# A two-slope rectifier in place for narrowing float64 weights, and 128 columns instead of 80 in the stationary operands of counts and means

## The chip, the core and the metric

The kernel runs on one core of one Trainium2 chip. The time is that of one execution on the device, in microseconds (us); smaller is better.

The names used for the engines: PE is TensorE (matrix multiplications; its weight loads are listed apart as PEld), DVE is VectorE, ACT is ScalarE, POOL is GpSimd, SP is SyncE, which here only issues DMA transfers. SBUF is the on-chip working memory, PSUM the small memory that PE writes its results into.

## The reference

Three stages follow each other. The first is an attention over 16 (batch, head) pairs of 768 positions and 64 dimensions, in which a query sees only the keys of its own cluster. A query whose cluster has no key gets the mean of v. The second is a gated feed-forward layer, the third a soft mixture of experts.

```python
q_assign = np.argmax(np.einsum('bhsd,hcd->bhsc', q_n, c_n), axis=-1)
k_assign = np.argmax(np.einsum('bhsd,hcd->bhsc', k_n, c_n), axis=-1)
mask = q_assign[:, :, :, None] == k_assign[:, :, None, :]
scores = np.where(mask, scale * np.matmul(q, k.transpose(0, 1, 3, 2)), -1000000000.0)
attn = np.exp(scores - np.max(scores, axis=-1, keepdims=True))
attn = attn / (np.sum(attn, axis=-1, keepdims=True) + 1e-09)
x = np.matmul(attn, v)                       # reshaped to 1536 x 512
...
h = x @ w_in                                 # 1536 x 2048
g = h * np.clip(h + 3.0, 0.0, 6.0) / 6.0
x = g @ w_out
...
logits = x @ phi                             # dispatch and combine by softmax of logits,
h = np.maximum(slot_input[e] @ w1[e], 0.0)   # 8 experts with 4 slots each
slot_out[e] = h @ w2[e]
```

`w_in` (512 x 2048) and `w_out` (2048 x 512) reach the kernel as float64, two 32-bit words a number. PE multiplies float16 and float32, so the kernel first narrows them to float32.

## The kernel before, in words

The work is written as generators that yield at places where another step may come in between; the table `ORDER` (lines 29 to 132) says by number which generator goes on next. All engines thus get one fixed sequence of instructions, and each engine works through its own strictly in that order. A second table, `ROOMS`, gives each tile its buffer.

**Attention, heads 0 to 15.** For each head: q and k are loaded and split into a high and a low float16 half (`cast_hi`, `cast_lo`), clusters are found (`as_mm`, `as_max`; the one-hot rows of keys and queries stand in the tile `oh`), the row maxima are taken from a first product (`maxq` on PE, line 531, then `maxr` on DVE, line 547, and `shift`, lines 554 and 556), the scores are formed (`scores`, lines 569 and 573), exponentiated on ACT (`exps`, lines 610 and 617), split (ACT line 342, POOL line 352, which the helpers `high` and `low` issue) and multiplied by v (`pv`, lines 639, 644, 645 and 652).

**Counts and means** (`cnt_mm`, lines 497 to 525), once for each head. Six products count the keys of each cluster (line 505: the stationary operand is a stretch of 5 x 16 = 80 columns of `oh`, the moving one a column of ones), and twelve form the mean of v (lines 507 and 508: the stationary operand is `wmean`, 80 columns, zero but for the last 16). Only rows 64 to 79 of the result are read.

**Narrowing** (`narrow`, lines 870 to 891), for 16 pieces of 128 x 1024 numbers: 8 of `w_in` (tile `wi`, through `win`) and 8 of `w_out` (tile `wod`, through `wout`). A piece lies in a buffer of `ring_a` (4 buffers), low and high words alternating. Its steps:

- part 0: DVE masks the sign out of the high words into the tile `nw` (line 878); ACT takes the absolute value of the high words, seen as float32, times 2 to the -111, into a PSUM tile `nt` (line 880). `nt` takes one of the three two-bank buffers of PSUM that the scores, maxima and hidden products also use.
- part 1: DVE shifts `nt` left by 3 and ors in the sign (line 883).
- part 2: DVE shifts the low words right by 29, ors in `nt` and writes the float32 (line 888). For `w_in` that is in place, then ACT and POOL split it (`wq`); for `w_out` it goes to `wo`, from which ACT issues a DMA (line 935), and the buffer of the piece is then free for the next load (line 922, on SP).

**The rest.** The hidden products (`hid`, line 710) of the first batch are interleaved with the attention of the second; after the attention its buffers are given to the experts' weights (`wk`), whose transfers run until the end.

The `consts` steps (lines 309 to 338) fill constants on POOL at the start.

Of the kernel before, what the change touches and what calls it, by code (L numbers as in the profile page):

```python
# [8 lines left out]
F16 = mybir.dt.float16  # L9
F32 = mybir.dt.float32  # L10
U32 = mybir.dt.uint32
I32 = mybir.dt.int32
AF = mybir.ActivationFunctionType
ALU = mybir.AluOpType
# [3 lines left out]
P = 128  # L18
# [213 lines left out]
def clustered_attention_ffn_softmoe(ctx: ExitStack, tc, q, k, v, cent, w_in, w_out, phi, w1, w2, out):  # L232
    nc = tc.nc
    B, H, S, D = q.shape
    C = cent.shape[1]
    NT = S // P
# [11 lines left out]
    cp = Rooms(ctx.enter_context(tc.tile_pool(name="cp", bufs=1, side="left")))  # L248
# [6 lines left out]
    ap = Rooms(att.enter_context(tc.tile_pool(name="ap", bufs=2, side="left")))  # L255
# [5 lines left out]
    def psm(nm):  # L261
        return ps_m.tile([P, 512], F32, tag="m", name=nm)

    def pss(nm):
        return ps_s.tile([P, 2, 512], F32, tag="s", name=nm)
# [17 lines left out]
    ident16 = cp.tile([P, P], F16, name="ident16")  # L283
    i4 = cp.tile([P, NS], F32, name="i4")
    ones = cp.tile([P, 1], F16, name="ones")
    wmean = cp.tile([P, 80], F16, name="wmean")
    rank = cp.tile([P, C], F32, name="rank")
    b_relu = cp.tile([P, 1], F32, name="b_relu")
    wp2 = cp.tile([P, NF, 2 * NS], F16, name="wp2")
# [11 lines left out]
    v32s = [ap.tile([P, NT, 65], F32, name=f"v32_{i}", bufs=1) for i in range(3)]  # L301
    mxs = [ap.tile([P, 96 + NT], F32, name=f"mxs_{i}", bufs=1) for i in range(2)]
    mvs = [ap.tile([P, 129], F16, name=f"mv_{i}", bufs=1) for i in range(3)]

    def second():
        nc.scalar.activation(sm.tile([P, 1], F32, tag="nm", name="warm_1", bufs=4), b_relu, AF.Exp)
        yield

    def consts():
        make_identity(nc, ident)  # L310
        nc.gpsimd.tensor_copy(ident16, ident)  # L311
        yield
        for c in range(C):
            nc.gpsimd.memset(rank[:, c : c + 1], float(C - c))
        yield
        for t in qk2:
            nc.gpsimd.memset(t[:, :, :, 80:128], 0.0)
            nc.gpsimd.memset(t[:, :, 1, 96 : 96 + NT], SH)
            yield
# [144 lines left out]
    def as_max(i):  # L464

        d = st[i]
        sc = d.pop("as")
        rk = rank.unsqueeze(1).to_broadcast([P, 12, C])
        nc.vector.tensor_tensor(out=sc, in0=sc, in1=rk, op=ALU.mult)
        yield  # L470
        mx2 = sm.tile([P, 12], F32, tag="mx2", name=f"mx2_{i}", bufs=2)
        nc.vector.tensor_reduce(out=mx2, in_=sc, op=ALU.max, axis=AX.X)
        oh = ap.tile([P, 2, NT, C], F16, tag="oh", name=f"oh_{i}")
        nc.vector.tensor_tensor(
            out=oh.rearrange("p a n c -> p n a c"),
            in0=sc.rearrange("p (n a) c -> p n a c", a=2),
            in1=mx2.rearrange("p (n a) -> p n a", a=2).unsqueeze(3).to_broadcast([P, NT, 2, C]),
            op=ALU.is_equal,
        )
        d["oh"] = oh  # L480
# [16 lines left out]
    def cnt_mm(i):  # L497

        d = st[i]
        oh = d["oh"]  # L500
        v1 = v1s[i % NV]
        pm = psm(f"cm_{i}")
        for n in range(NT):
            k5 = oh.rearrange("p a n c -> p (a n) c")[:, NT + n - 4 : NT + n + 1].rearrange("p n c -> p (n c)")
            nc.tensor.matmul(pm[0:80, 400:401], k5, ones, start=(n == 0), stop=(n == NT - 1))
        for n in range(NT):
            nc.tensor.matmul(pm[0:80, 0:65], wmean, v1[:, n, 0:65], start=(n == 0), stop=False)
            nc.tensor.matmul(pm[0:80, 0:64], wmean, v1[:, n, 65:129], start=False, stop=(n == NT - 1))
        yield
        emp = sm.tile([P, 1], F32, tag="emp", name=f"emp_{i}", bufs=2)  # L510
        nc.vector.tensor_scalar(out=emp[64:80], in0=pm[64:80, 400:401], scalar1=0.5, scalar2=None, op0=ALU.is_lt)
        yield
        d["cm"] = pm
        mv = mvs[i % 3]
        nc.vector.tensor_scalar(
            out=mv[64:80, 0:65], in0=pm[64:80, 0:65], scalar1=emp[64:80], scalar2=None, op0=ALU.mult
        )
        nc.vector.scalar_tensor_tensor(  # L518
            out=mv[64:80, 65:129],
            in0=pm[64:80, 0:64],  # L520
            scalar=emp[64:80],
            in1=mv[64:80, 0:64],
            op0=ALU.mult,
            op1=ALU.subtract,
        )
# [307 lines left out]
    def centroids():  # L833
        c32 = ap.tile([P, D], F32, tag="acp", name="c32", bufs=1)
        nc.scalar.dma_start(out=c32, in_=cent.rearrange("h c d -> (h c) d"))
        nc.gpsimd.memset(b_relu, 3.0 * SG)
        nc.scalar.activation(sm.tile([P, 1], F32, tag="nm", name="warm_0", bufs=4), b_relu, AF.Sqrt)
        yield
        sq = ap.tile([P, D], F32, tag="oh", name="csq")
        ss = sm.tile([P, 1], F32, tag="tm", name="css")  # L840
        nc.scalar.activation(sq, c32, AF.Square, accum_out=ss)
        y = sm.tile([P, 1], F32, tag="tm", name="cy")
        nc.scalar.activation(y, ss, AF.Sqrt)
        yield
        nc.vector.tensor_scalar(out=y, in0=y, scalar1=1e-20, scalar2=None, op0=ALU.max)
        r = sm.tile([P, 1], F32, tag="tm", name="cr")
        nc.vector.reciprocal(r, y)
        nc.vector.scalar_tensor_tensor(out=y, in0=ss, scalar=r, in1=y, op0=ALU.mult, op1=ALU.add)
        nc.vector.tensor_scalar(out=y, in0=y, scalar1=0.5, scalar2=1e-6, op0=ALU.mult, op1=ALU.add)
        nc.vector.reciprocal(r, y)  # L850
        cn = ap.tile([P, D], F32, tag="oh", name="cn")
        nc.vector.tensor_scalar(out=cn, in0=c32, scalar1=r, scalar2=SQ, op0=ALU.mult, op1=ALU.mult)
        cin = ap.tile([P, 4, D], F16, tag="ms", name="cin", bufs=1)
        cb = cn.unsqueeze(1).to_broadcast([P, 2, D])
        nc.vector.tensor_copy(cin[:, 0:2], cb)
        nc.vector.tensor_tensor(out=cin[:, 2:4], in0=cb, in1=cin[:, 0:2], op=ALU.subtract)
        yield
        tp = psm("ctp").bitcast(F16)[:, 0 : 2 * P].rearrange("p (a q) -> p a q", a=2)
        for a in range(2):
            nc.tensor.transpose(tp[:, a], cin[:, 2 * a : 2 * a + 2].rearrange("p a d -> p (a d)"), ident16)  # L860
        yield
        nc.vector.tensor_copy(ct, tp)
# [4 lines left out]
    raw = {}  # L867
    wo = {}

    def narrow(dst, src, nm, part):  # L870

        lo, hi = src[:, :, 0], src[:, :, 1]
        if part == 0:
            t = raw[nm, "t"] = pss(f"nt_{nm}").rearrange("p a b -> p (a b)").bitcast(U32)
            s = raw[nm, "s"] = ap.tile([P, 1024], U32, tag="nw", name=f"nw_{nm}", bufs=1)
            nc.vector.tensor_scalar(out=s, in0=hi, scalar1=0x80000000, scalar2=None, op0=ALU.bitwise_and)
            yield
            nc.scalar.activation(t.bitcast(F32), hi.bitcast(F32), AF.Abs, scale=2.0**-111)  # L880
        elif part == 1:
            t = raw[nm, "t"]
            nc.vector.scalar_tensor_tensor(
                out=t, in0=t, scalar=3, in1=raw.pop((nm, "s")), op0=ALU.logical_shift_left, op1=ALU.bitwise_or
            )
        else:
            t = raw.pop((nm, "t"))
            nc.vector.scalar_tensor_tensor(
                out=dst.bitcast(U32), in0=lo, scalar=29, in1=t, op0=ALU.logical_shift_right, op1=ALU.bitwise_or
            )  # L890
        yield

# [163 lines left out]
    def phs_load():  # L1056
        nc.sync.dma_start(out=phs, in_=phi.rearrange("(k p) s -> p k s", p=P))
        yield

    ev(consts)  # L1060
    for n in range(7):
        ev(keep, n, 4)
    ev(centroids)
    ev(load, 0, 0)
    ev(load, 0, 1)
# [4 lines left out]
    for i in range(NH):  # L1070
        if i == H:
            for t in range(NT):
                ev(xtrans, t)
        if i >= 2:
            ev(load, i, 0)
        if i:
            ev(load, i, 1)
        for fn in (cast_hi, cast_lo, as_mm, as_max, as_put, castv_hi, castv_lo, cnt_mm):
            ev(fn, i)
        for n in range(NT):  # L1080
            ev(maxq, i, n)
            ev(maxr, i, n)
        ev(shift, i)
        for t in range(NT):
            ev(scores, i, t)
            ev(exps, i, t)
            ev(plow, i, t)
            ev(pv, i, t)
        ev(finish, i)
        ev(split_x, i)  # L1090
# [387 lines left out]
```

## Time and profile before

| What | Value |
|---|---|
| Time, median of 3 runs | 478.05 us (477.79 to 480.21) |
| The profiled execution, first to last instruction (its span; no other time of it is recorded) | 475.5 us |
| PE busy | 437.2 us, 92% |
| ACT busy | 316.9 us, 67% |
| DVE busy | 284.3 us, 60% |
| POOL busy | 251.1 us, 53% |
| Chain that ended last, by engine | PE 66%, DVE 14%, ACT 8%, DMA 6% |

The profile follows one execution on the chip. Busy times are shares of the whole span, so they average stages that have different limits; a change in one stage is read from that stage. The chain of waits goes back from the last instruction, at each step to what released it or to the instruction before it on its engine. The ends of matrix products are modelled, so a PE that looks busy may still wait in part; the starts show the pace.

### The profile page before, as it was taken

Reading aid. Unit: us, or ns where it says so; the run is one execution under the profiler, and the core shown is the slowest. Engines: PE = TensorE matmul, PEld = TensorE weight load, DVE = VectorE, ACT = ScalarE, POOL = GpSimd, SP = SyncE. Lnnn points to the kernel's source line nnn. Section 1 sums busy time; section 2 is a strip of 40 time slices with the busy share of each in tenths; the row PEclk is TensorE's granted clock in tenths of the full one; section 3 lists DMA queues with packets and bytes.
Section 4 is the critical chain, followed back from the end, with each engine's and each line's share of the span. In section 5 each row is a group of like instructions: output and inputs, shape, how many; then the busy total and the mean of one; then the engine's idle time right before and its main releaser. Section 6 shows DMA issues by size and latency. Waiting matters only on the chain.

```text
span 475.5 us, 11894 instructions
## 1 busy us (share of the span) xinstructions
PE 437.2 (92%) x4938; PEld 283.1 (60%) x4938; DVE 284.3 (60%) x497; ACT 316.9 (67%) x518; POOL 251.1 (53%) x227
## 2 busy tenths in 40 slices
PE   6779999999979999999999998989998999789973
PEld 5557678777767656656666666754545545442443
DVE  4899999998968387466667759513233223540222
ACT  7369899898965978876789998963545335600121
POOL 5326588785644555666698897984313233130000
PEclk9789999999999999999999999999999999999998
DMA  8777866946794689689473555005996799999998
GB/s 280 187 150 187 193 172 174 271 122 196 244 253 113 177 203 195 139 157 226 112 145 72 54 102 139 3 1 106 314 307 207 158 274 373 406 341 384 339 284 272
DMA packets 133813, 95.50 MB, mean 201 GB/s; under 512 B 96384, under 2 KB 119424, under 8 KB 133760
## 3 DMA queue, kind: packets, MB, share of 16 engines
q1 hardware_dynamic: 129088, 88.95, 71.2%
q10 hardware_dynamic: 4672, 5.80, 3.4%
q8 instruction: 38, 0.62, 0.5%
q14 instruction: 15, 0.12, 0.1%
HBM read 64.06 MB, written 7.34 MB: 150 GB/s over the span
## 4 chain that ended last, share of the span: by engine, by line
PE 66%; DVE 14%; ACT 8%; DMA 6%; issue 3%; POOL 2%; SPq 0%; ACTq 0%; DVEq 0%; POOLq 0%
PE h L710 26%; DVE mxs L547 4%; PE st L569 4%; PE sm L531 4%; PE st L573 4%; PE e L1345 3%; DMA wod<-in_moe_w_out_dram 3%; PE acc L639 2%; PE acc L652 2%; PE z L819 2%; DMA wk<-in_moe_w_dram 2%; ACT p L617 2%; PE acc L645 2%; PE acc L644 2%; PE o L1382 2%
## 5 line engine op out<-in xcount | busy, mean ns | idle before, releaser
L352 POOL TENSOR_TENSOR pp<-p,pp 128x768 f16<-128x768 f32 x72 | 119.7, 1667 | 56.1 <-ACT pp L342 28.0
L710 PE MATMUL h<-wq,xt 128*128 128x512 f16 x576 | 132.1, 379 | 0.0
L547 DVE TENSOR_REDUCE mxs<-sm 128x1 f32<-128x768 f32 x96 | 89.5, 952 | 15.7 <-PE sm L531 15.0
L710 PEld LDWEIGHTS <-xt 128*128 128x128 f16 x576 | 55.2, 98 | 62.0 <-issue 2.5
L352 POOL TENSOR_TENSOR ghl<-r,ghl 128x1024 f16<-128x1024 f32 (+1 forms) x25 | 50.4, 2017 | 61.1 <-ACT ghl L342 55.9
L617 ACT ACTIVATE p<-st 128x768 f32<-128x768 f32 x72 | 57.9, 805 | 15.2 <-PE st L573 13.7
L342 ACT ACTIVATE pp<-p 128x768 f16<-128x768 f32 x72 | 60.3, 842 | 1.4 <-PE acc L652 0.2
L569 PE MATMUL st<-qk1t 128*128 128x384 f16 x192 | 47.6, 329 | 5.5 <-ACT p L617 4.9
L531 PE MATMUL sm<-qk2t 80*128 80x384 f16 x192 | 45.9, 331 | 2.7 <-DVE mxs L547 0.9
L729 DVE SCALAR_TENSOR_TENSOR r<-r,h 128x1024 f32<-128x1024 f32 (+1 forms) x26 | 29.5, 1135 | 31.4 <-ACT r L727 31.3
L573 PE MATMUL st<-qk2t 102*128 102x384 f16 x192 | 47.5, 329 | 0.0
L727 ACT ACTIVATE r<-h,b_relu 128x1024 f32<-128x1024 f32 (+1 forms) x26 | 27.2, 1045 | 24.7 <-PE h L710 13.8
L645 PE MATMUL acc<-v,pp 128*128 128x64 f16 x432 | 36.1, 194 | 0.0
L644 PE MATMUL acc<-v,pp 128*128 128x65 f16 x432 | 36.1, 192 | 0.0
L352 POOL TENSOR_TENSOR qk<-qk,qk 128x768 f16<-128x768 f32 x15 | 24.7, 1645 | 21.7 <-ACT qk L342 20.5
L639 PE MATMUL acc<-v,pp 128*128 128x65 f32 x288 | 35.8, 274 | 0.3 <-DVE wp L973 0.2
L639 PEld LDWEIGHTS acc<-v,pp 128*128 128x128 f32 x288 | 34.6, 192 | 1.5 <-DVE mv L518 0.3
L342 ACT ACTIVATE ghl<-r 128x1024 f16<-128x1024 f32 (+1 forms) x26 | 25.7, 989 | 14.3 <-DVE r L729 10.5
L644 PEld LDWEIGHTS <-pp 128*128 128x128 f16 x432 | 31.2, 99 | 2.5 <-ACT pp L342 0.2
L645 PEld LDWEIGHTS <-pp 128*128 128x128 f16 x432 | 29.2, 96 | 2.1
L342 ACT ACTIVATE qk<-qk 128x768 f32<-128x768 f32 (+2 forms) x32 | 26.2, 817 | 1.8 <-DMA qk<-in_k_dram 0.9
L361 PE MATMUL kw<-ident,ident 128*128 128x256 f16 x136 | 23.4, 306 | 4.0 <-POOL ident L311 1.8
(195 smaller groups left out, 785.3 us busy)
## 6 DMA issues: line engine op xcount, KB each, us to landing
wk<-in_moe_w_dram SPq DMA_DIRECT2D x60, 512.0 KB, 8.2
wi<-in_moe_w_in_dram SPq DMA_DIRECT2D x16, 512.0 KB, 5.7
wod<-in_moe_w_out_dram SPq DMA_DIRECT2D x16, 512.0 KB, 5.2
wos<-wo ACTq DMA_DIRECT2D x8, 512.0 KB, 3.2
wk<-wos SPq DMA_DIRECT2D x8, 512.0 KB, 6.6
qk<-in_q_dram SPq DMA_DIRECT2D x16, 192.0 KB, 3.0
qk<-in_k_dram SPq DMA_DIRECT2D x16, 192.0 KB, 3.5
v<-in_v_dram SPq DMA_DIRECT2D x16, 192.0 KB, 3.5
```

The lines of the kernel that those rows point to most:

```text
L342: nc.scalar.activation(out, in_, AF.Copy, scale=scale)
L352: (nc.vector if e == "v" else nc.gpsimd).tensor_tensor(out=out, in0=in_, in1=hi, op=ALU.subtract)
L531: nc.tensor.matmul(s[:, j, 0:384], d["qk2t"][0:80, n, 0], d["qk2t"][0:80, 3 * j : 3 * j + 3, 1], start=True, stop=True,)
L547: nc.vector.tensor_reduce(out=mxs[i % 2][:, 96 + n : 97 + n], in_=s[:, :, 0:384], op=ALU.max, axis=AX.XY)
L569: nc.tensor.matmul(s[:, j, 0:384], d["qk1t"][:, t, 1], d["qk1t"][:, 3 * j : 3 * j + 3, 0], start=True, stop=False)
L573: nc.tensor.matmul(s[:, j, 0:384], d["qk2t"][0 : 96 + NT, t, 1], d["qk2t"][0 : 96 + NT, 3 * j : 3 * j + 3, 0], start=False, stop=True,)
L617: nc.scalar.activation(p32, s[:, :, 0:384], AF.Exp, scale=sc_exp)
L639: nc.tensor.matmul(o, p32[:, j, r * P : (r + 1) * P], d["v32"][:, t], start=(t == 0 and n == 0), stop=False)
L644: nc.tensor.matmul(o, hi, v1[:, t, 0:65], start=(t == 0 and n == 0), stop=False)
L645: nc.tensor.matmul(o[:, 0:64], hi, v1[:, t, 65:129], start=False, stop=False)
L710: nc.tensor.matmul(s[:, fb % 2], xt[:, lhs], wq[fb][:, hl, kk], start=(n == 0), stop=(n == 11))
L729: nc.vector.scalar_tensor_tensor(out=g, in0=r, scalar=6.0 * SG, in1=sf, op0=ALU.min, op1=ALU.mult)
```

## The change

`narrow` loses the tiles `nw` and `nt` and one DVE instruction of three. Part 0 is now a shift of the low words right by 29 in place on DVE, and a two-slope rectifier (`Prelu`) of the high words in place on ACT, with the scale 2 to the -111 and the slope 2 to the 32 for negative inputs: the factor adds 32 to the exponent field, a bit that the later shift by 3 brings to the place of the sign. Part 1 does nothing. Part 2 shifts the high words left by 3 and ors in the low ones. `cnt_mm` uses stationary operands of 128 columns: the one-hot rows lie in two fixed tiles `ohs` with four zero groups behind the twelve, and `wmean` is 128 wide. POOL zeroes these with two more `memset`s. `ORDER` is not touched.

```diff
-    wmean = cp.tile([P, 80], F16, name="wmean")
+    wmean = cp.tile([P, P], F16, name="wmean")
...
+    ohs = [ap.tile([P, 16, C], F16, name=f"ohs_{i}", bufs=1) for i in range(2)]
...
             nc.gpsimd.memset(rank[:, c : c + 1], float(C - c))
+        for t in ohs:
+            nc.gpsimd.memset(t[:, 12:16], 0.0)
...
-        oh = ap.tile([P, 2, NT, C], F16, tag="oh", name=f"oh_{i}")
+        oh = ohs[i % 2][:, 0:12].rearrange("p (a n) c -> p a n c", a=2)
...
-        oh = d["oh"]
+        oh = ohs[i % 2]
         v1 = v1s[i % NV]
         pm = psm(f"cm_{i}")
         for n in range(NT):
-            k5 = oh.rearrange("p a n c -> p (a n) c")[:, NT + n - 4 : NT + n + 1].rearrange("p n c -> p (n c)")
-            nc.tensor.matmul(pm[0:80, 400:401], k5, ones, start=(n == 0), stop=(n == NT - 1))
+            k8 = oh[:, NT + n - 4 : NT + n + 4].rearrange("p n c -> p (n c)")
+            nc.tensor.matmul(pm[:, 400:401], k8, ones, start=(n == 0), stop=(n == NT - 1))
         for n in range(NT):
-            nc.tensor.matmul(pm[0:80, 0:65], wmean, v1[:, n, 0:65], start=(n == 0), stop=False)
-            nc.tensor.matmul(pm[0:80, 0:64], wmean, v1[:, n, 65:129], start=False, stop=(n == NT - 1))
+            nc.tensor.matmul(pm[:, 0:65], wmean, v1[:, n, 0:65], start=(n == 0), stop=False)
+            nc.tensor.matmul(pm[:, 0:64], wmean, v1[:, n, 65:129], start=False, stop=(n == NT - 1))
...
-        sq = ap.tile([P, D], F32, tag="oh", name="csq")
+        sq = ap.tile([P, D], F32, tag="csq", name="csq", bufs=1)
...
-        cn = ap.tile([P, D], F32, tag="oh", name="cn")
+        cn = ap.tile([P, D], F32, tag="cn", name="cn", bufs=1)
...
         if part == 0:
-            t = raw[nm, "t"] = pss(f"nt_{nm}").rearrange("p a b -> p (a b)").bitcast(U32)
-            s = raw[nm, "s"] = ap.tile([P, 1024], U32, tag="nw", name=f"nw_{nm}", bufs=1)
-            nc.vector.tensor_scalar(out=s, in0=hi, scalar1=0x80000000, scalar2=None, op0=ALU.bitwise_and)
+            nc.vector.tensor_scalar(out=lo, in0=lo, scalar1=29, scalar2=None, op0=ALU.logical_shift_right)
             yield
-            nc.scalar.activation(t.bitcast(F32), hi.bitcast(F32), AF.Abs, scale=2.0**-111)
-        elif part == 1:
-            t = raw[nm, "t"]
+            h = hi.bitcast(F32)
+            nc.scalar.activation(h, h, AF.Prelu, scale=2.0**-111, alpha=2.0**32)
+        elif part == 2:
             nc.vector.scalar_tensor_tensor(
-                out=t, in0=t, scalar=3, in1=raw.pop((nm, "s")), op0=ALU.logical_shift_left, op1=ALU.bitwise_or
-            )
-        else:
-            t = raw.pop((nm, "t"))
-            nc.vector.scalar_tensor_tensor(
-                out=dst.bitcast(U32), in0=lo, scalar=29, in1=t, op0=ALU.logical_shift_right, op1=ALU.bitwise_or
+                out=dst.bitcast(U32), in0=hi, scalar=3, in1=lo, op0=ALU.logical_shift_left, op1=ALU.bitwise_or
             )
         yield
```

On DVE the sequence stays as it was but for the 16 instructions of line 883. The stretch below is from the middle of the first batch's attention, where two pieces of `w_in` are narrowed close together (`wi` the piece, `nt` and `nw` its helper tiles, `mxs` the row maxima, `emp` and `mv` the counts and means). Before:

```order
L547 TENSOR_REDUCE mxs_113<-sm_0_1184 128x1
L883 SCALAR_TENSOR_TENSOR nt_i_0_1100<-nt_i_0_1100,nw_i_0_1101 128x1024
L511 TENSOR_SCALAR emp_1210<-cm_1191 16x1
L888 SCALAR_TENSOR_TENSOR wi_0_1097<-wi_0_1097,nt_i_0_1100 128x1024
L878 TENSOR_SCALAR nw_i_1_1236<-wi_1_1216 128x1024
L515 TENSOR_SCALAR mv_116<-cm_1191,emp_1210 16x65
L518 SCALAR_TENSOR_TENSOR mv_116<-cm_1191,emp_1210,mv_116 16x64
L883 SCALAR_TENSOR_TENSOR nt_i_1_1235<-nt_i_1_1235,nw_i_1_1236 128x1024
L888 SCALAR_TENSOR_TENSOR wi_1_1216<-wi_1_1216,nt_i_1_1235 128x1024
```

With the change, the same place on DVE (the lines are numbered anew: 879 is the shift of part 0, 884 the last step):

```order
L550 TENSOR_REDUCE mxs_113<-sm_0_1169 128x1
L514 TENSOR_SCALAR emp_1194<-cm_1175 16x1
L884 SCALAR_TENSOR_TENSOR wi_0_1084<-wi_0_1084 128x1024
L879 TENSOR_SCALAR wi_1_1200<-wi_1_1200 128x1024
L518 TENSOR_SCALAR mv_116<-cm_1175,emp_1194 16x65
L521 SCALAR_TENSOR_TENSOR mv_116<-cm_1175,emp_1194,mv_116 16x64
L884 SCALAR_TENSOR_TENSOR wi_1_1200<-wi_1_1200 128x1024
```

Nothing else moved: the two instructions of line 883 are gone, and both inputs of the last step now lie in `wi`, which is in SBUF, where one of them was `nt`. ACT issues the same instructions in the same order, with no table load added; PE too, with 128 columns in `cnt_mm`.

## Rows read from the trace of the kernel before

**Rows 1.** Busy us of each engine (instructions) by stage; then granted PE clock, DMA share, GB/s.
```profile
18.00:40.00 22.00, 19.43 (x159) 13.02 (x157) 19.98 (x36) 13.40 (x24) 4.98 (x4) 0.84 0.59 136
40.00:130.00 90.00, 85.81 (x1049) 68.33 (x1048) 84.76 (x133) 83.41 (x124) 68.21 (x47) 1.00 0.75 199
130.00:157.00 27.00, 24.17 (x287) 19.78 (x286) 19.47 (x32) 17.36 (x25) 12.08 (x8) 0.94 0.61 169
157.00:290.00 133.00, 132.88 (x1549) 83.05 (x1547) 85.56 (x154) 112.62 (x187) 96.96 (x62) 1.00 0.74 147
```

**Rows 2.** Chain that ended last, in order of time: start us, us, what.
```profile
26.84 1.15 DVE nt_i L883
28.01 0.97 DVE qk2t L556
...
125.71 1.14 DVE nt_o L883
...
131.87 7.25 DMA wod<-in_moe_w_out_dram
```

**Rows 3.** Single lines: instructions of `narrow` on DVE; ns min/median/max, first and last start.
```profile
L878 DVE TENSOR_SCALAR nw_i<-wi x8: 681/685/1932, 10.2 to 119.3; 128x1024 uint32<-128x1024 uint32 x8
L883 DVE SCALAR_TENSOR_TENSOR nt_i<-nt_i,nw_i x8: 1220/1223/1232, 14.3 to 120.8; 128x1024 uint32<-128x1024 uint32 x8
```

**Rows 4.** Timeline of ACT, at 139 us: start us, us, what [idle before].
```profile
139.23 1.10 ACT L880 ACTIVATE nt_o<-wod 128x1024 f32<-128x1024 f32 x1 [3.23 <-DMA wod<-in_moe_w_out_dram]
```

**Rows 5.** Timelines of DVE and POOL, where one meets the other.
```profile
10.18 1.93 DVE L878 TENSOR_SCALAR nw_i<-wi 128x1024 uint32<-128x1024 uint32 x1 [2.21 <-DMA wi<-in_moe_w_in_dram]
9.93 1.64 POOL L352 TENSOR_TENSOR qk<-qk,qk 128x768 f16<-128x768 f32 x1 [3.93 <-ACT qk L342]
65.46 0.69 DVE L878 TENSOR_SCALAR nw_i<-wi 128x1024 uint32<-128x1024 uint32 x1
65.65 2.01 POOL L352 TENSOR_TENSOR pp<-p,pp 128x768 f16<-128x768 f32 x1 [0.53 <-POOL pp L352]
```

**Rows 6.** The same, first and last instruction of line 888 that finds POOL busy.
```profile
30.70 1.21 DVE L888 SCALAR_TENSOR_TENSOR wi<-wi,nt_i 128x1024 uint32<-128x1024 uint32 x1
30.31 1.65 POOL L352 TENSOR_TENSOR qk<-qk,qk 128x768 f16<-128x768 f32 x1 [3.14 <-ACT qk L342]
183.85 1.22 DVE L888 SCALAR_TENSOR_TENSOR wo<-wod,nt_o 128x1024 uint32<-128x1024 uint32 x1
182.19 2.29 POOL L352 TENSOR_TENSOR ghl<-r,ghl 128x1024 f16<-128x1024 f32 x1 [0.26 <-ACT ghl L342]
```

**Rows 7.** Timeline of DVE: two instructions with both inputs in SBUF.
```profile
3.99 1.11 DVE L350 SCALAR_TENSOR_TENSOR qk<-qk,qk 128x384 f16<-128x384 f32 x2 [3.99 <-ACT qk L342]
```

**Rows 8.** Single lines of ACT: into PSUM, and from the same `wi` into SBUF.
```profile
L880 ACT ACTIVATE nt_i<-wi x8: 1072/1097/1158, 10.2 to 119.3; 128x1024 f32<-128x1024 f32 x8
L342 ACT ACTIVATE wq<-wi x8: 1122/1130/1150, 45.0 to 131.5; 128x1024 f16<-128x1024 f32 x8
```

**Rows 9.** Timeline of PE: one head's counts and means, what follows, and 128-column products.
```profile
303.63 0.36 PE L505 MATMUL cm<-ones,oh 128*80 128x1 f16 x6
303.85 0.20 PE L507 MATMUL cm<-v,wmean 128*80 128x65 f16 x1
...
304.31 0.20 PE L644 MATMUL acc<-v,pp 128*128 128x65 f16 x1
...
304.68 0.34 PE L652 MATMUL acc<-v,pp 128*128 128x65 f16 x6
...
37.38 0.46 PE L445 MATMUL as<-ct,qk1t 128*128 128x32 f16 x12
```

**Rows 10.** Weight loads by line and shape: busy us, mean ns; idle before.
```profile
L644 PEld LDWEIGHTS <-pp 128*128 128x128 f16 x432 | 31.2, 99 | 2.5 <-ACT pp L342 0.2
L507 PEld LDWEIGHTS <-wmean 128*80 128x80 f16 x96 | 8.4, 127 | 0.0
```

**Rows 11.** Timeline of POOL at the start.
```profile
4.57 1.21 POOL L419 COPY qk<-qk 128x768 f16<-128x768 f16 x1 [1.07 <-ACT qk L342]
```

## The prediction

> **What bounds the kernel now.** I read busy time by stage first [rows 1]. From 157 to 290 us PE is busy for 132.88 of 133 us: there only cheaper PE work counts. Ahead of that no engine stands out. From 40 to 130 us PE is busy for 85.81 of 90 us, DVE for 84.76, ACT for 83.41, so that the idle times are 4.2, 5.2 and 6.6 us; from 18 to 40 us DVE is the fullest with 19.98 of 22; from 130 to 157 us PE has 24.17 of 27, at a granted clock of 0.94. Who of three nearly full engines sets the pace is read from the chain of waits [rows 2]. Between 26 and 127 us seven of the sixteen instructions of line 883 lie on it, the first with 1.15 us at 26.84, the last with 1.14 at 125.71, 8.4 us in all; right behind the first stands line 556, without which no score of that head can start. At 131.87 the chain passes through the load of a piece of `w_out`, which had to wait for a buffer that line 888 frees; ACT stood idle for it for 3.23 us [rows 4].
>
> What follows the attention starts when its buffers come free, so I let a gain made before 157 us come through to the end in full.
>
> **The instruction that goes.** Sixteen times 1.22 us [rows 3] are 19.6 us of DVE time. On the path lie at most the 8.4 us of the chain. PE's idle time in the three stages before 157 us bounds it too: 2.6 + 4.2 + 2.8 = 9.6 us [rows 1], and into this goes whatever ACT gains by no longer needing a PSUM buffer for `nt`. The low end is nothing: ACT, next in line, has only 6.6 us to spare in 90.
>
> **The shift of part 0.** Line 878 takes 0.685 us [rows 3], with a strided input in SBUF; the shift has the same input and differs in its strided output. I take 0.685. The far end is the pace of line 883, 1.22: 16 times 0.54, or 8.6 us of DVE time more.
>
> **The last step, now all in SBUF.** Alone it should cost what it did: two instructions with both inputs in SBUF take 1.11 us for 384 elements each [rows 7], 0.56 apiece, and the further 640 elements at about one a nanosecond give 1.2 us. Beside POOL it may not. Line 888 has one input in PSUM and takes 1.21 us though POOL is in the middle of an instruction of 1.65 [rows 6]; these two don't heed each other. Line 878 lies wholly in SBUF, and there they do [rows 5]: at 10.18 it takes 1.93 us, till just behind the end of POOL's instruction (9.93 + 1.64), and at 65.46, where DVE was first, POOL's takes 2.01 us instead of 1.64. No row shows an instruction with two SBUF inputs beside a busy POOL. Its price lies between nothing and the rest of POOL's instruction each time: ten of the sixteen instructions of line 888 find POOL busy, the first and the last in [rows 6], with 1.3 and 0.6 us to go, 12.1 us in all. That would give back 62% of the 19.6 us. [Rows 5] are nearest, so I expect most of it.
>
> The Trainium skill says in "SBUF — State Buffer", section "Who interferes with whom", that a VectorE instruction with two SBUF inputs and a GpSimd instruction that reads SBUF exclude each other, and that whichever issues first keeps the other waiting to its end. For VectorE's faster modes [rows 5] agree; for two inputs no run here shows it. By that rule the gain of the chain would be 38% of 8.4, or 3.2 us, and without it 8.4.
>
> So the narrowing gives between 3.2 and 8.4 us where DVE sets the pace. I take 4.5, closer to the low end, because of [rows 5] and because ACT and PE are so close behind.
>
> **ACT.** The rectifier writes into SBUF, line 880 into PSUM. From the same `wi`, ACT takes 1.10 us into PSUM and 1.13 into SBUF [rows 8]: 0.03 us, sixteen times 0.5 us, of which I count 0.3 on the path. For the rectifier itself there is no row; that line 880 spreads from 1.07 to 1.16 us gives what I allow, 0.09 us each, 1.4 in all, either way.
>
> **Counts and means.** For one head the six products of line 505 run from 303.63 to 303.85 and the twelve of lines 507 and 508 to 304.31: 37 and 38 ns from start to start [rows 9]. The next twelve, with the same widths but 128 stationary columns, need 0.37 us, 31 ns each. For line 505 the nearest 128-column products are those of line 445: twelve span 0.46 us where six of line 505 span 0.36, and without the some 0.18 us of the last one that is 25 ns against 36. What differs is the weight load: 99 ns with 128 columns, 127 with 80 [rows 10]. So a head saves 0.09 + 0.07 = 0.16 us, sixteen heads 2.5. Half of the heads have these products after 157 us, where PE sets the pace: 1.25 us surely. Of the other half I count one half, 0.6.
>
> **Fills on POOL.** The added columns, 176 in all, are a quarter of the 768 that the copy in [rows 11] treats in 1.21 us: 0.3 us, ahead of an idle time of 1.07 us. I cost them at nothing; with that cover gone they delay this copy by 0.3 us.
>
> **The sum.** 4.5 + 1.9 - 0.3 = 6.1 us. The span of the profiled execution would fall from 475.5 to 469.4 us. The median of the three runs stands 2.5 us above that span, and I carry this over: 478.05 - 6.1 = 472.0 us. A measurement of this kernel can tell about 0.5%, or 2.4 us, from no change: 475.7 to 480.4 us.
>
> **Rivals.**
> - More comes free. If DVE and POOL leave each other alone, the whole 8.4 us go and all 2.5 of the counts, and the 131.87 load comes early enough to lift the 0.94 clock of its stage, worth up to 0.06 of 27 us, of which I count 0.6: 466.5 us. For it: DVE pieces follow each other on the chain. Against it: [rows 5].
> - The gain is hidden. ACT and PE take DVE's place at once and only the 1.25 us of the late heads remain: 476.8 us. For it: idle times of 4.2 and 6.6 in 90 us. The shift at 1.22 us would lead here as well.
> - Slower, by the meeting of DVE and POOL. The place is line 352 on POOL against the new last step. It decides when a piece waits for more than the 1.22 us that it saves. If all sixteen wait for a whole 1.65 us, DVE gains nothing and loses 6.8 us; at the chain's share of 8.4 in 19.6 that is 2.9 on the path. The ten pieces that hold POOL up for 1.22 us would cost it 12.2 us; at the same share, and halved since POOL has 21.8 of 90 us idle [rows 1], 2.6. With 1.25 back: 482.3 us. For it: ten meetings. Against it: the average rest is 0.75 us a piece, not 1.65.
> - The wider operands don't load faster. If the load grew with its columns, 127 ns would become 203, the pace of 38 ns 61, and 288 products cost 6.6 us more: 3.3 in the late heads and half of the rest, 5.0. Against the 4.2 of the narrowing: 478.9 us. Against it: [rows 9, 10].
>
> The Trainium skill gives that rule in "TensorE: Matmul & The Clock Gate", section "LDWEIGHTS (loading the stationary operand)": the time of a load goes with its columns. [Rows 10] go the other way.
>
> **Chances.** My forecast (469 to 475.7 us) 0.54; more comes free 0.12; hidden 0.22; slower by DVE and POOL 0.09; loads not faster 0.03. Faster by over 0.5%: 0.54 + 0.12 = 0.66. Within 0.5%: 0.22 + 0.03 = 0.25. Slower: 0.09. The range goes from 466.5, the whole chain, to 478.2 us, which takes in the hidden case with a shift that is dearer than taken; outside lie the slower rival, the last one and the far side of the first, under 0.2 together.
>
> **What would show it.** Right: no instruction of line 883; the new last step longer than 1.3 us on average, or a late start of POOL's instructions beside it; the twelve products of the means in some 0.37 us and weight loads near 99 ns; scores of the second head starting earlier by about 1 us behind line 556; PE's start into its full stretch (157 us) earlier by 4 to 5 us. Wrong: last steps at 1.22 us throughout with POOL undisturbed (the first rival); PE's full stretch beginning where it did (the second); last steps above 2 us and longer waits of line 652 for POOL (the third); loads above 127 ns (the fourth); a shift above 1 us wherever POOL is idle.

## The result, and the profile after

The changed kernel took 480.11 us (median of 12 runs) against 477.92 us for the kernel before (12 runs): ratio 1.0062, 95% interval 1.0034 to 1.0089. A second series (e15) gave 1.0079 (1.0048 to 1.0109). The ratios go by the fast runs alone, without those more than 1.5% above the fastest of their kernel, so that they are not the quotients of the medians. The kernel is slower, where I had forecast 472.0 us. The profiled execution took 478.82 us, with a span of 476.7 us.

The page's line of busy times:

```profile
PE 436.1 (91%) x4938; PEld 281.0 (59%) x4938; DVE 275.3 (58%) x481; ACT 317.3 (67%) x518; POOL 259.6 (54%) x229
```

Sixteen instructions of 1.22 us went from DVE, 19.6 us, but its busy time fell by 9.0 only, from 284.3, and POOL's rose by 8.5, from 251.1, though it has only two fills more. The stages of [rows 1], now (busy us of PE, weight loads, DVE, ACT, POOL; then granted clock, DMA share, GB/s):

```profile
18.00:40.00 22.00, 19.12 (x162) 12.88 (x161) 18.85 (x35) 13.87 (x24) 6.93 (x4) 0.89 0.73 174
40.00:130.00 90.00, 82.97 (x1017) 65.77 (x1016) 79.89 (x122) 81.15 (x121) 72.41 (x46) 1.00 0.71 189
130.00:157.00 27.00, 24.18 (x290) 19.50 (x288) 17.59 (x29) 17.14 (x26) 12.51 (x9) 0.94 0.65 181
157.00:290.00 133.00, 132.12 (x1546) 82.15 (x1544) 84.66 (x152) 113.01 (x186) 97.23 (x62) 1.00 0.72 145
```

From 40 to 130 us PE, DVE and ACT all do less in the same 90 us than before, and POOL alone is busy for longer. The two DVE lines of `narrow` (ns min/median/max, first and last start):

```profile
L879 DVE TENSOR_SCALAR wi<-wi x8: 685/690/1876, 10.1 to 120.1; 128x1024 uint32<-128x1024 uint32 x8
L879 DVE TENSOR_SCALAR wod<-wod x8: 685/698/1410, 94.0 to 182.4; 128x1024 uint32<-128x1024 uint32 x8
...
L884 DVE SCALAR_TENSOR_TENSOR wi<-wi x8: 1216/1336/2310, 13.0 to 122.4; 128x1024 uint32<-128x1024 uint32 x8
L884 DVE SCALAR_TENSOR_TENSOR wo<-wod x8: 1215/1384/2958, 101.2 to 183.7; 128x1024 uint32<-128x1024 uint32 x8
```

Undisturbed, the shift takes 0.685 us and the last step 1.22. Added up over the sixteen pieces the last step takes 26.1 us, 6.7 above sixteen undisturbed ones; line 888 took 19.5. The shift takes 15.4; line 878 took 12.6. What they wait for stands in the timeline. DVE at 71 us:

```profile
71.89 2.31 DVE L884 SCALAR_TENSOR_TENSOR wi<-wi 128x1024 uint32<-128x1024 uint32 x1
74.11 0.69 DVE L879 TENSOR_SCALAR wi<-wi 128x1024 uint32<-128x1024 uint32 x1
...
75.47 1.93 DVE L884 SCALAR_TENSOR_TENSOR wi<-wi 128x1024 uint32<-128x1024 uint32 x1
```

and POOL beside it:

```profile
70.97 2.13 POOL L355 TENSOR_TENSOR wq<-wi,wq 128x1024 f16<-128x1024 f32 x1
74.45 1.87 POOL L355 TENSOR_TENSOR pp<-p,pp 128x768 f16<-128x768 f32 x1 [1.34 <-issue]
76.28 3.13 POOL L355 TENSOR_TENSOR wq<-wi,wq 128x1024 f16<-128x1024 f32 x1
```

POOL's first instruction ends at 73.10; the last step, issued at 71.89, ends 1.10 us behind that, a little less than its own length. The second one, issued at 75.47 with 0.85 us of POOL's `pp` to go, ends at 77.40, 1.08 behind; and the `wq` that POOL had issued at 76.28 takes 3.13 us instead of 2.15, because it in turn waits until about 77.3. Each engine waits for the other's instruction to its end. At 101 us two such waits follow each other on DVE:

```profile
101.18 2.65 DVE L884 SCALAR_TENSOR_TENSOR wo<-wod 128x1024 uint32<-128x1024 uint32 x1 [0.91 <-POOL wq L355]
103.75 0.35 DVE L472 TENSOR_TENSOR as<-as,rank 128x192 f32<-128x192 f32 x1
104.01 1.88 DVE L879 TENSOR_SCALAR wi<-wi 128x1024 uint32<-128x1024 uint32 x1
105.81 0.94 DVE L550 TENSOR_REDUCE mxs<-sm 128x1 f32<-128x768 f32 x1
```

POOL then had `pp` from 101.10 for 1.64 us and from 103.23 for 2.10. The row maxima behind them are what PE waits for:

```profile
106.80 0.49 PE L572 MATMUL st<-qk1t 128*128 128x384 f16 x2 [1.27 <-DVE mxs L550]
```

I set each PE product's start in the two traces against the other's, product for product. The changed kernel leads by 1.2 us until 106 us. It loses 1.4 at the row above, 0.7 at 112 and 0.8 at 122, and is 1.2 us late at 157, 1.5 at the end. These places are those of one execution. In the profiled execution of e15, the same kernel, the step that meets POOL at 101 us here runs beside an idle POOL; PE loses 3.2 us at an earlier place instead (94 to 98 us of the kernel before), where ACT waits 2.47 us for a load of `k` and PE's granted clock then falls to 0.66 (from 98 to 100 us); it ends 1.2 us late all the same. In the first execution the chain of waits passes the same places (start us, us, what):

```profile
99.03 2.12 POOL wq L355
...
104.22 6.45 DMA wod<-in_moe_w_out_dram
...
113.73 1.75 DVE wo L884
...
120.14 1.46 DVE wi L879
```

POOL's `wq` and the slowed shift and last step stand where line 883 stood in [rows 2].

### The profile page after: what moved, and what is told of

It is laid out like the page before. It is cut to its first block, busy times and chain, and to the rows that moved or that the text cites. A ratio compares the mean times of both kernels' runs of the same rounds, so it can differ in the third digit from the quotient of the medians.

```text
span 476.7 us, 11880 instructions
## 1 busy us (share of the span) xinstructions
PE 436.1 (91%) x4938; PEld 281.0 (59%) x4938; DVE 275.3 (58%) x481; ACT 317.3 (67%) x518; POOL 259.6 (54%) x229
## 4 chain that ended last, share of the span: by engine, by line
PE 55%; ACT 10%; DMA 10%; DVE 9%; issue 5%; POOL 3%; SPq 2%; DVEq 0%; POOLq 0%; ACTq 0%
PE h L713 23%; PE sm L534 3%; PE st L572 3%; DVE mxs L550 3%; PE st L576 3%; DMA wod<-in_moe_w_out_dram 3%; PE e L1341 3%; ACT p L620 3%; DMA qk2t<-qk 2%; ACT pp L345 2%; SPq L1015 2%; PE o L1378 2%; DMA qk<-in_k_dram 1%; PE z L822 1%; PE acc L642 1%
## 5 line engine op out<-in xcount | busy, mean ns | idle before, releaser
L355 POOL TENSOR_TENSOR pp<-p,pp 128x768 f16<-128x768 f32 x72 | 121.7, 1695 | 54.4 <-ACT pp L345 32.4
L355 POOL TENSOR_TENSOR qk<-qk,qk 128x768 f16<-128x768 f32 x15 | 27.6, 1842 | 22.9 <-ACT qk L345 22.2
L345 ACT ACTIVATE ghl<-r 128x1024 f16<-128x1024 f32 (+1 forms) x26 | 25.7, 988 | 14.3 <-DVE r L732 10.5
L534 PEld LDWEIGHTS <-qk2t 80*128 80x128 f16 x192 | 17.2, 100 | 17.1 <-issue 6.7
L345 ACT ACTIVATE qk<-qk 128x768 f32<-128x768 f32 (+2 forms) x32 | 26.1, 817 | 1.7 <-DMA qk<-in_q_dram 0.8
```

The lines of the kernel that those rows point to most:

```text
L345: nc.scalar.activation(out, in_, AF.Copy, scale=scale)
L355: (nc.vector if e == "v" else nc.gpsimd).tensor_tensor(out=out, in0=in_, in1=hi, op=ALU.subtract)
L534: nc.tensor.matmul(s[:, j, 0:384], d["qk2t"][0:80, n, 0], d["qk2t"][0:80, 3 * j : 3 * j + 3, 1], start=True, stop=True,)
```

## The experiments

Theory A: the new last step, with two SBUF inputs, and POOL wait for each other, and this gives back the gain. Theory B: the gain is hidden behind ACT and PE, and the meeting costs nothing on the path. Theory C: the wider operands cost. All results (DVE and POOL: busy us of the profiled execution):

| Kernel | Median us | Ratio to before (95%) | DVE | POOL |
|---|---|---|---|---|
| full change | 480.11 | 1.0062 (1.0034 to 1.0089) | 275.3 | 259.6 |
| e15_full_again | 479.15 | 1.0079 (1.0048 to 1.0109) | 274.8 | 260.2 |
| e2_narrow | 478.73 | 1.0019 (0.9987 to 1.0051) | 275.1 | 259.1 |
| e6_counts | 476.85 | 1.0015 (0.9984 to 1.0046) | 285.7 | 251.6 |
| e3_psum | 471.08 | 0.9882 (0.9845 to 0.9920) | 266.5 | 250.6 |
| e7_psum_80 | 470.46 | 0.9869 (0.9837 to 0.9902) | 266.4 | 250.2 |
| e5_shift_psum | 471.49 | 0.9895 (0.9860 to 0.9931) | 273.1 | 248.8 |
| e4_sbuf_nt | 500.79 | 1.0509 (1.0467 to 1.0550) | 301.6 | 264.5 |
| e8_dve_dose | 474.81 | 0.9961 (0.9929 to 0.9994) | 275.9 | 250.4 |
| e9_pool_dose | 478.73 | 1.0031 (1.0001 to 1.0062) | 272.4 | 267.8 |
| e10_pool_dose | 473.12 | 0.9911 (0.9880 to 0.9941) | 273.7 | 257.2 |
| e11_dve_dose | 476.94 | 0.9986 (0.9959 to 1.0012) | 281.8 | 249.0 |
| e12_both | 477.78 | 1.0009 (0.9986 to 1.0033) | 282.0 | 257.2 |
| e13_dve_waits | 474.90 | 0.9991 (0.9963 to 1.0018) | 275.0 | 250.9 |
| e14_both_waits | 476.44 | 1.0028 (0.9994 to 1.0061) | 275.8 | 259.5 |

They ran in four sets, on different chips; each ratio is to the kernel before on the same chip, and kernels of different sets are compared by it.

**The two parts apart.** Each is one part of the diff on the kernel before: e2 has `narrow`, e6 has `ohs` and `wmean`.

```diff
 e2_narrow:  the edits in narrow only
 e6_counts:  the edits of wmean, ohs, cnt_mm and the tags of csq and cn only
```

> The kernel before with the new narrowing alone; counts and means keep 80 columns. Theory A (the meeting with POOL: the new last step has two SBUF inputs, waits for the POOL instruction that is under way, and holds up the next one): the last step takes 1.5 to 1.8 us on average against 1.21 alone, each wait equal to the rest of POOL's instruction; POOL is busy for 256 to 261 us against 251.1; the time is 479 to 485 us, slower than before by 0.2 to 1.4%, and some 1 us above the full change. Theory C (the 128-column operands are what costs): this kernel is faster than before, 473 to 477 us.

> The kernel before with the 128-column counts and means alone; its narrowing is kept. From the trace of the full change, where each late head gains 0.10 to 0.15 us on PE: sixteen heads save at most 2.4 us, and the time is 475 to 477 us, 0.998 to 0.994 of before. Rival (the wider operands are the cost, or the added fills are): slower than before, 479 us or more.

In e2 the last step takes 1.65 us on average and POOL is busy for 259.1 us, as theory A has it; the time, 0.2% above before, lies just below its range, and below the full change, where I had expected it 1 us above. Neither part alone can be told from no change. For e6 that is a miss: 0.994 to 0.998 was expected, and the interval begins at 0.9984. Theory C is taken up with e7 below.

**One input in PSUM.** Two ways to give the last step one input in each memory:

```diff
 e3_psum, against the full change:
+            t = raw[nm, "t"] = pss(f"nt_{nm}").rearrange("p a b -> p (a b)").bitcast(U32)
...
-            h = hi.bitcast(F32)
-            nc.scalar.activation(h, h, AF.Prelu, scale=2.0**-111, alpha=2.0**32)
+            nc.scalar.activation(t.bitcast(F32), hi.bitcast(F32), AF.Prelu, scale=2.0**-111, alpha=2.0**32)
...
-                out=dst.bitcast(U32), in0=hi, scalar=3, in1=lo, ...
+                out=dst.bitcast(U32), in0=t, scalar=3, in1=lo, ...

 e5_shift_psum, against the full change:
+        elif part == 1:
+            nc.vector.tensor_scalar(out=raw[nm, "t"], in0=lo, scalar1=29, scalar2=None, op0=ALU.logical_shift_right)
...
-                out=dst.bitcast(U32), in0=hi, scalar=3, in1=lo, ...
+                out=dst.bitcast(U32), in0=hi, scalar=3, in1=t, ...
```

> The full change, but the rectifier writes to a PSUM tile as the absolute value did before, so that the last step has one input in PSUM and one in SBUF. Theory A: the last step takes 1.20 to 1.24 us all sixteen times, beside a busy POOL too; POOL is busy for 250 to 254 us; the 19.6 us of the removed instruction are kept on DVE, and the time is 472 to 477 us, faster than before by 0.2 to 1.2%. Theory B (the gain is hidden behind ACT and PE, the meeting costs nothing on the path): within 0.3% of the full change, 478.5 to 481.5 us. Theory C: above 479 us too, with POOL undisturbed.

> The full change, but it is the shift that writes to PSUM, at the place in DVE's order where the removed instruction stood, and the rectifier stays in place in SBUF. The last step again has one input in PSUM. Theory A: the last step takes 1.20 to 1.24 us throughout; if an SBUF-to-SBUF single-input instruction in its fast form is what heeds POOL, the shift too has one duration all sixteen times, between 0.68 and 1.22 us. At 0.7 the time is 472 to 476 us; at 1.2 it gives back 8 us of DVE time and the time is 475 to 479 us. Theory B: 478.5 to 481.5 us, as the full change.

Both are 1.1 to 1.2% faster than before, e3 a little more than theory A said; B is out, and C is left to e7. Since e5 keeps the rectifier in SBUF, it is not the rectifier's output that costs. The last steps of e3, and the timelines of DVE and POOL at the place shown above:

```profile
L885 DVE SCALAR_TENSOR_TENSOR wi<-nt_i,wi x8: 1212/1216/1250, 12.9 to 116.7; 128x1024 uint32<-128x1024 uint32 x8
L885 DVE SCALAR_TENSOR_TENSOR wo<-nt_o,wod x8: 1212/1224/1225, 99.6 to 174.3; 128x1024 uint32<-128x1024 uint32 x8
```

```profile
69.93 1.23 DVE L885 SCALAR_TENSOR_TENSOR wi<-nt_i,wi 128x1024 uint32<-128x1024 uint32 x1
71.07 0.98 DVE L880 TENSOR_SCALAR wi<-wi 128x1024 uint32<-128x1024 uint32 x1
```

```profile
69.34 2.15 POOL L355 TENSOR_TENSOR wq<-wi,wq 128x1024 f16<-128x1024 f32 x1
```

The last step runs through beside `wq`, which keeps its 2.15 us. The shift behind it, all in SBUF, still waits: it takes 0.98 us, until 0.56 behind the end of `wq`. In e5 the shift writes to PSUM:

```profile
L884 DVE TENSOR_SCALAR nt_i<-wi x8: 1216/1220/1229, 11.5 to 113.8; 128x1024 uint32<-128x1024 uint32 x8
```

It heeds POOL no more, and pays with 1.22 us instead of 0.685. I had expected 475 to 479 us at that price; the 6.6 us more of DVE time against e3 don't show in the time. The shift's meetings, which e5 is rid of, and its later place in DVE's order may pay for them; no run keeps the two apart.

From 130 to 157 us e3 gains most at one place. Its stages (columns as above):

```profile
40.00:130.00 90.00, 86.54 (x1064) 68.94 (x1064) 75.82 (x127) 84.37 (x126) 66.06 (x47) 1.00 0.76 200
130.00:157.00 27.00, 26.86 (x286) 19.67 (x285) 16.49 (x29) 21.21 (x35) 15.34 (x11) 1.00 0.81 212
```

ACT waits there for the piece of `w_out` of [rows 4], 3.06 us in the full change and 0.17 in e3 (e3 first):

```profile
132.22 1.15 ACT L882 ACTIVATE nt_o<-wod 128x1024 f32<-128x1024 f32 x1 [0.17 <-DMA wod<-in_moe_w_out_dram]
```

```profile
140.38 1.15 ACT L882 ACTIVATE wod<-wod 128x1024 f32<-128x1024 f32 x1 [3.06 <-DMA wod<-in_moe_w_out_dram]
```

From 140 to 150 us (full change, then e3):

```profile
140.00:150.00 10.00, 7.73 (x72) 5.66 (x72) 5.58 (x11) 7.35 (x9) 3.24 (x2) 0.83 0.68 190
```

```profile
140.00:150.00 10.00, 9.87 (x126) 8.18 (x125) 7.25 (x10) 6.21 (x9) 3.45 (x3) 1.00 0.47 131
```

By PE's starts the full change is 1.6 us behind e3 at 95 us of e3's time, 5.3 at 132, and 9.7 at 137: 4.5 us fall at this load, in PE's pause and in a granted clock of 0.83 behind it (a mean over the levels 1.2 and 2.4 GHz), where e3 keeps 1.00. At the end 8.0 are left, since e3 has the lower clock later on, 0.83 from 410 to 425 us against 1.00 in the full change:

```profile
410.00:425.00 15.00, 13.66 (x136) 5.06 (x136) 5.58 (x14) 0.52 (x1) 4.31 (x26) 0.83 0.87 317
```

But this load is not what makes one kernel better than another. ACT waits for it in e5, which is as fast as e3, and PE's clock falls there too; in e15, the full change again, the clock stays up and the time is no better (ACT's row and the stage, e5 and then e15):

```profile
132.53 1.14 ACT L882 ACTIVATE wod<-wod 128x1024 f32<-128x1024 f32 x1 [2.54 <-DMA wod<-in_moe_w_out_dram]
130.00:157.00 27.00, 24.72 (x261) 17.72 (x260) 15.59 (x26) 17.74 (x27) 11.43 (x10) 0.94 0.67 169
```

```profile
142.36 1.18 ACT L882 ACTIVATE wod<-wod 128x1024 f32<-128x1024 f32 x1 [2.84 <-DMA wod<-in_moe_w_out_dram]
130.00:157.00 27.00, 24.37 (x313) 20.22 (x312) 19.06 (x31) 18.78 (x29) 13.84 (x8) 1.00 0.67 184
```

e5 has its lead ahead of this load: by PE's starts it is 6.0 us ahead of before at 130 us, where e3 is 4.0 ahead; both are 6.4 ahead at the end.

**The counts in the faster kernel.** Before with e3's `narrow` and 80 columns:

```diff
 e7_psum_80, against the kernel before:
 the edits of e3_psum in narrow only
```

> The new narrowing with its rectifier into PSUM, as in e3_psum, but counts and means with 80 columns. If the meetings with POOL were all that was wrong with the narrowing, it keeps what e3_psum gained but for the counts' 1 to 2.5 us: 472 to 474 us. Rival (the gain of e3_psum came from the counts, in a kernel in which PE is now more often the bound): 475 us or more.

Ratio 0.9869 against e3's 0.9882, faster than expected: the gain does not come from the counts, and theory C falls as what costs. That the wider operands cost a little is not excluded: in each pair the kernel that has them is the slower one, by 0.1 points (e6 over before, e3 over e7) and by 0.4 to 0.6 (full change and e15 over e2), where the intervals still overlap.

**More of it.** The kernel before, with line 880 in place:

```diff
 e4_sbuf_nt, against the kernel before:
-            t = raw[nm, "t"] = pss(f"nt_{nm}").rearrange("p a b -> p (a b)").bitcast(U32)
+            t = raw[nm, "t"] = hi
```

> The kernel before, all its instructions kept, but the absolute value goes back into its own input in SBUF instead of PSUM: thirty-two DVE steps now have two SBUF inputs, where the full change has sixteen. ACT has no PSUM buffer to wait for, but has to wait for the mask. Theory A: both steps take 1.4 us or more on average, POOL's busy time rises to 258 to 270 us, and the time is 482 to 492 us, slower than before and than the full change. Theory B: the time is 476 to 480 us, since ACT's waits for PSUM buffers go and the meetings don't reach the path.

```profile
L883 DVE SCALAR_TENSOR_TENSOR wi<-wi,nw_i x8: 1215/1306/2435, 14.4 to 132.9; 128x1024 uint32<-128x1024 uint32 x8
...
L888 DVE SCALAR_TENSOR_TENSOR wi<-wi x8: 1226/1519/2550, 15.6 to 134.3; 128x1024 uint32<-128x1024 uint32 x8
```

The side was right and the size too small: 5.1% slower, some 24 us, for 17.3 us more on DVE and 13.4 on POOL; the two steps take 1.39 and 1.81 us on average. By the doses below that lost time would cost about half of the 24 us (an estimate). ACT must also wait for the mask here, which this run does not keep apart.

**Which engine's lost time counts.** Doses without the meetings:

```diff
 e8_dve_dose (on e3_psum) and e11_dve_dose (on e5_shift_psum), ahead of the last step:
+            nc.vector.tensor_scalar(out=t[:, 0:384], in0=t[:, 0:384], scalar1=0, scalar2=None, op0=ALU.bitwise_or)
 e9_pool_dose (on e3_psum, 1152 elements) and e10_pool_dose (on e5_shift_psum, 576):
+            nc.gpsimd.memset(spare, 0.0)
 e12_both: both, on e5_shift_psum
```

> e3_psum with one more DVE instruction ahead of each last step, which ORs 0 into 384 elements of the PSUM tile: about 0.58 us, sixteen times, 9.3 us of DVE time, as much as the full change loses on DVE to the meetings; POOL is not held up by it. Theory A1 (what costs is DVE's own waiting): 478 to 482 us, as the full change. Theory A2 (DVE's waits are half of it, POOL's being held up the other): 473.5 to 477 us. Theory A3 (only POOL's being held up costs): 470.5 to 472.5 us.

> e3_psum with one more POOL instruction ahead of each last step, a fill of 1152 elements of a tile that nobody reads: 0.57 us, sixteen times, 9.2 us of POOL time, as much as the full change holds POOL up; DVE's last steps should stay at 1.22 us. Theory A1 (what costs is DVE's own waiting): 470.5 to 472.5 us. Theory A2 (both count): 473 to 477 us. Theory A3 (POOL's being held up is what costs): 478 to 482 us.

> e9_pool_dose mended: its fill took 1.06 us instead of 0.57, and the shift, which there is an SBUF-to-SBUF instruction in the fast form, waited for it. This is e5_shift_psum, in which no DVE step of the narrowing heeds POOL, with a fill of 576 elements on POOL ahead of each last step: some 0.53 us, sixteen times, 8.5 us of POOL time, close to the 9.0 that the full change holds POOL up for; DVE's steps stay at 1.22 us. Theory A1 (what costs is DVE's own waiting): 470.5 to 473 us, within 0.3% of e5_shift_psum. Theory A2 (POOL's being held up is about half of the loss): 474 to 477 us. Theory A3 (it is all of it): 478 to 482 us.

> e5_shift_psum with the extra DVE instruction of e8_dve_dose: 0.56 us, sixteen times, 9.0 us of DVE time, POOL untouched. Theory A2: as in e8_dve_dose, some 0.8% above the kernel without it, 473.5 to 477 us. Theory A1: 478 to 482 us. Theory A3: 470.5 to 473 us.

> e5_shift_psum with both doses, 9.0 us on DVE and 8.5 on POOL, and no instruction that waits for the other engine's. If occupied time on the two engines is all that the meetings cost, this is as slow as the full change: 478.5 to 482 us, 1.003 to 1.009 of before. If the coupling itself costs (the two engines made to take turns), it stays faster: 473 to 477 us.

9 us on DVE cost 0.8 and 0.9 points (e8 over e3, e11 over e5), 8.4 on POOL 0.2 (e10), which is less than the intervals resolve, and both 1.1 (e12). A1 falls with e8 and e11, A3 with e10, but the halves of A2 look unequal, with DVE's waits the dearer; in what proportion, intervals of some 0.3 points either way leave open. e9 missed as a dose: its fills take 1.06 us, and the shift waited for them too, so that DVE lost 5.9 us as well. The full change loses 1.8 points on e3; e12 falls short of that, between its two expectations.

**The waits at their places.** Even doses are not where the waits were, so I put them back piece by piece:

```diff
 e13_dve_waits, on e3_psum (elements per piece, in order):
+    WAIT_SHIFT = [0, 0, 0, 0, 175, 0, 0, 960, 0, 580, 90, 545, 0, 0, 0, 0]
+    WAIT_LAST = [[], [], [50], [], [930], [540], [1024, 32], [], [357], [400], [], [], [], [143], [], [1024, 350]]
...
+                nc.vector.tensor_reduce(out=spare, in_=hi.bitcast(F32)[:, 0:n], op=ALU.max, axis=AX.X)
...
+                nc.vector.tensor_scalar(out=t[:, 0:n], in0=t[:, 0:n], scalar1=0, scalar2=None, op0=ALU.bitwise_or)
 e14_both_waits: also, ahead of thirteen of line 355's instructions on POOL
+                    nc.gpsimd.memset(fill[:, 0:n], 0.0)
```

> e3_psum with DVE's waits put back piece by piece instead of as an even dose: ahead of each last step and each shift that waited for POOL in the trace of the full change, a DVE instruction of about that wait's length (eight last steps, 0.2 to 1.7 us, 6.6 in all; five shifts, 0.25 to 1.15 us, 3.2 in all), none ahead of the others; nothing is added on POOL. If it matters where DVE's waits fall and they carry the loss: 478 to 482 us, as the full change. If only their sum matters: 473.5 to 476.5 us, as e8_dve_dose.

> e13_dve_waits, and POOL's hold-ups put back too: ahead of the thirteen POOL instructions that were held up in the full change a fill of that length (0.2 to 1.1 us, 9.1 in all). If the two engines' lost time, at its places, is the whole of it: 478.5 to 482 us, 1.002 to 1.009 of before, as the full change. If taking turns costs something of its own: below 478 us.

> The full change itself, on the same chip as the two kernels that imitate it, since the question is one of half a per cent: 1.003 to 1.009 of before, 478.5 to 482 us.

Over e3's 0.9882, DVE's waits at their places cost 1.1 points, POOL's hold-ups 0.4 more, and 0.5 remain to e15, whose interval meets e14's. In us e13 lies in the range for a mere sum; by its ratio it lies between its two cases, 0.3 points above e8, which the intervals do not separate. Whether the places matter is so left open. So about three quarters of the loss is the lost time of the two engines, most of it DVE's; whether the last quarter is a price of the coupling or an inexact imitation (a fill cannot be held up in turn) stays open. With 80 columns the whole loss is 1.5 points (e2 over e7), no more than e14 puts back.

e3_psum, e5_shift_psum and e7_psum_80 beat both kernels. Which of the three is best can't be told.

## Why the prediction was wrong, point by point

- **What bounds the kernel.** Right in the place: by PE's starts e3, e5 and e7 are 8.1, 6.7 and 8.1 us ahead of before at 157 us. That such a gain comes through in full is not quite so: 6.4, 6.4 and 7.3 us are left at the end.
- **The instruction that goes.** Right: none is left, and where nothing else gets in its way this is worth 1.2 to 1.3% (e3, e7), 5.6 to 6.3 us, inside the 3.2 to 8.4 us that I took for the narrowing. I had taken 4.5 for the case with the meetings; it fits the case without.
- **The shift of part 0.** 0.685 us is right for it alone. But I read from [rows 5] that an instruction of this form waits for POOL and then priced it as if it met POOL no more often than line 878: 15.4 us against 12.6. In e3, beside a last step that no longer waits, the same shift takes 12.6.
- **The last step.** The mechanism was right: 1.22 us alone, and beside POOL the rest of POOL's instruction and then some 1.1 us. The bound on DVE's wait was on the safe side, 12.1 us against 6.7 measured, though its sum is off: it comes out only if two of POOL's instructions from 120.76 us on are counted as one. Instruction by instruction the ten rests are 10.5 us, or 53%, and the low end is 3.9 us in place of 3.2, which does not help the forecast. **The step that failed is the price put on the meetings**: "That would give back 62% of the 19.6 us", and so "the gain of the chain would be 38% of 8.4, or 3.2 us". I let the waits shrink the gain in proportion, so that it could not go below nothing, and with 4.5 of 8.4 us I charged them 3.9. They cost 1.5 to 2.0 points, 7 to 9 us (e2 over e7; full change and e15 over e3), more than the 5.6 to 6.3 that the removed instruction gives. The waits are a loss of their own: put back on DVE alone, 8.5 to 9.4 us cost 0.8 to 1.1 points, 4 to 5 us (e8, e11, e13). And outside of a rival I charged nothing for POOL's being held up, 8.5 us, which costs 0.2 to 0.4 points more by e10 and e14, less than the intervals resolve. A lost microsecond of DVE was thus worth 0.4 to 0.6 at the end, a saved one about 0.3; whether the two differ, and whether by the places of the waits, the runs leave open.
- **ACT.** 1.16 us on average against 1.11 for line 880, 0.8 us in all: taken 0.3 on the path, allowed up to 1.4. Into PSUM the same rectifier takes 1.12 (e3).
- **Counts and means.** The load fell to 99 ns as said, and a head takes 0.54 us where it took 0.68 [rows 9, 10]: 0.14 saved, 0.16 said. Timeline of PE (twelve products from 305.04, the next tile at 305.43), and the load:

```profile
304.89 0.29 PE L508 MATMUL cm<-ones,ohs 128*128 128x1 f16 x6
305.04 0.19 PE L510 MATMUL cm<-v,wmean 128*128 128x65 f16 x1
...
305.43 0.19 PE L647 MATMUL acc<-v,pp 128*128 128x65 f16 x1
```

```profile
L510 PEld LDWEIGHTS <-wmean 128*128 128x128 f16 x96 | 6.8, 99 | 0.0
```

  Of the 1.9 us in the sum nothing shows at the end, the 1.25 "surely" included (e7, and e6, whose interval allows at most 0.8 us). In e6's profiled execution PE's lead over before grows from 2.4 us at 168 to 2.9 at 293, by 0.5 over these heads, and is 2.0 at the end.
- **Rivals.** The third, DVE and POOL, is what happened: its place and side were right, 482.3 us said, 480.1 measured. That the number comes so near is luck: it let all sixteen pieces wait for 1.65 us, 26.4 in all, where 6.7 were measured, and took 0.43 us at the end for each microsecond of DVE, where the runs show 0.4 to 0.6. Its condition was wrong. I let it decide only when a piece waits for more than the 1.22 us that it saves; two of the sixteen do, the average is 0.42, and it decided all the same. With ten meetings read from the trace 0.09 was too little for it. The first rival describes e3, but not its gain, 11.5 us said and 5.6 measured. In e3's profiled execution the chain gives 4.0 us up to the load at 131.87, where I had 8.4; the load and its clock, to which I gave 0.6, give 4.5; 2.0 are lost again behind 410 us, and the 2.5 of the counts don't show.
- **Signs.** The average last step of 1.63 us, the loads of 99 ns and the scores behind line 556, 2 us earlier, came as I had said for a right forecast; they show the mechanism and nothing of its price. The sign that could tell the price failed: PE is 1.2 us late at 157 us, not 4 to 5 early.
- **The Trainium skill** in "SBUF — State Buffer", section "Who interferes with whom", was borne out: the last step shows the waiting of both sides, in the rows at 71 to 77 us. That an operand in PSUM takes it away is shown by e3 and e5.

## What to carry to other kernels

Before moving an operand of a two-input DVE instruction from PSUM into SBUF, look at what POOL does at that time: keeping one input in PSUM was worth 1.5 to 2.0% here, more than the whole instruction that the change removed (1.2 to 1.3%). Price such a meeting on both engines, and as a loss of its own rather than as a discount on the gain, since its low end lies below nothing. Where three engines are nearly full, the time that goes from one of them is worth only a part of its length (here about three tenths).

## What the runs showed of the hardware that I had not expected

A fill on POOL, too, holds up a single-input instruction that lies wholly in SBUF, and may go ahead of one that is already waiting. In e9 (DVE, then POOL):

```profile
10.00 3.09 DVE L881 TENSOR_SCALAR wi<-wi 128x1024 uint32<-128x1024 uint32 x1 [2.05 <-DMA wi<-in_moe_w_in_dram]
```

```profile
9.90 1.64 POOL L355 TENSOR_TENSOR qk<-qk,qk 128x768 f16<-128x768 f32 x1 [3.93 <-ACT qk L345]
11.48 1.06 POOL L886 MEMSET spare<- 128x1152 f16 x1
12.50 1.35 POOL L355 TENSOR_TENSOR v<-v,v 128x384 f16<-128x384 f32 x1
```

The shift, issued at 10.00, ends at 13.09, 0.55 us behind the end of the fill and not of the instruction that it found. POOL's next instruction, 0.92 us elsewhere, then takes 1.35. Three more of e9's sixteen shifts wait through a fill that begins behind them, at 124.26, 128.93 and 183.66 us; they take 2.08 to 2.32 us.

Where ACT has to wait for the load of [rows 4], PE loses against e3 2.7 us if its granted clock stays at 1.00 (e15), and 3.9 to 4.5 if it falls to 0.83 behind the pause (e5, the full change and the kernel before). What decides between the two no run shows.
